# Batch 2's q in channel-major form, a new step list, and steps on other engines in an attention and gated-convolution kernel

## Chip, cores and metric

The kernel runs on 1 core of one Trainium2 chip. The metric is the device time of one execution in microseconds (us). A core has a matrix engine (PE, whose weight loads are shown apart as PEld), three elementwise engines (DVE, ACT, POOL) and SP, which here issues all the DMA transfers. Each engine takes its instructions strictly in the order of the program; engines wait for one another through semaphores.

## Reference

Eight batches, eight heads, 576 positions, 64 channels per head; everything is float32. A softmax of q over the channels of a head, a softmax of k over the positions, a 64x64 product per head, and then a causal convolution of five taps whose sigmoid gates a projection, followed by an output projection:

```python
q_s = np.exp(q - np.max(q, axis=-1, keepdims=True))
q_s = q_s / (np.sum(q_s, axis=-1, keepdims=True) + 1e-09)
k_s = np.exp(k - np.max(k, axis=2, keepdims=True))
k_s = k_s / (np.sum(k_s, axis=2, keepdims=True) + 1e-09)
kv = np.einsum('bhsd,bhse->bhde', k_s, v)
x = np.einsum('bhsd,bhde->bhse', q_s, kv)      # then (B, S, 512)
for j in range(5):
    gate_pre += conv_w[j][None, None, :] * xp[:, j:j + S, :]
gate = 1.0 / (1.0 + np.exp(-gate_pre))
out = (gate * (x @ w_val)) @ w_out
```

## The kernel before

The program is one list, ORDER (L31), of 973 steps such as "tap 1 3 0" (batch 1, block 3, tap 0). A loop at the end calls the function of each step, so the list alone sets the order of the instructions on every engine and of the DMAs on SP's queue. A letter at the end of a step names its engine: a is ACT, p is POOL, v is DVE. HOMES gives for each kind of buffer the sequence of buffers that its users take; a step that takes a buffer waits until all readers of its last user are done.

The 512 channels lie as 4 blocks of 128 partitions with the 576 positions along the free axis. Steps on PE, per batch: "kv b" (80 small matmuls), "attend b 0" and "attend b 1" (x of blocks 0, 1 and of blocks 2, 3), four "value b m" (24 matmuls each, x split into a high and a low part) and four "project b n" (24 matmuls each). PE writes to four PSUM banks, whose sequence is HOMES["bank"]. A bank is free again when its readers are done: for x they are x_high (L584), x_low (L597), first (L589), tap (L602) and far (L607); for a value block gated (L686); for a project block the copy to SBUF (L707). In a project the matmuls that need the block that was gated last come in the last quarter.

Between these: taps on DVE make the gate of a block, sigmoid (L616) on ACT, gated on DVE, then g_high and g_low split the product for project. x_low must have gone through all four blocks before the end of a batch's first value step, x_high before the parts that use it.

For q there are two ways. In batches 0, 1 and 2 q lies position-major; q_max, q_sub, q_exp, q_sum, q_eps, q_rec and q_mul normalise it, then PE transposes it (q_turn L542, 8 transposes each, twice a batch; tail_turn L556, 4 transposes for the last 64 positions of a pair of batches), and ACT copies it out (q_turned L553, tail_turned L562, tail_high L567). In batches 3 to 7 position-major q only yields the maximum plus the logarithm of the sum: q_total (L445, DVE), q_log (L451, ACT), l_turn (L455, one or two adds and four small transposes on DVE), l_row (L472, DMA to a row in DRAM), l_spread (L480, DMA of that row, repeated over partitions, into a buffer of q's kind). A second copy of q, channel-major from DRAM (load_qc L243), has this row subtracted (l_sub L488) and goes through the exponential (c_exp L492) straight into the form that attend reads. across (L240) says how many positions of a batch go this way: all 576 from batch 4 on, 512 in batch 3, whose last 64 come from the turn of the tail that batches 2 and 3 share.

At the start PE runs 24 warming matmuls (L724), while q and k of batch 0 and the packed weights (load_words, part, field, scaled, signed, joined, w_high, w_low: they unpack 64-bit words into two float parts) are made ready. The gates of blocks 0 and 1 of batch 0 are made on PE (conv, L663), which is the first long work after the warming.

## Time and profile before

| what | us |
|---|---|
| median of 3 runs (287.82 to 287.99) | 287.99 |
| the profiled execution | 287.65 |
| its span, first to last instruction | 285.9 |
| PE busy | 278.8 |
| PE weight loads busy | 250.6 |
| DVE busy | 231.7 |
| POOL busy | 205.8 |
| ACT busy | 192.8 |

The granted clock of PE was 1.00 throughout. Some 1.75 us of the profiled execution lie outside its span. Busy shares are averages over the span; the kernel has a start of about 27 us, a long middle in which all batches overlap, and a last part in which only PE has much to do. So the waits of PE and the share of each engine by stretch say more than the totals.

### The profile page before, as it was taken

To read this page: it belongs to the slowest core of one execution; us is meant where nothing else is said; L and a number is where in the kernel's file an instruction comes from. 1 tells how busy PE (TensorE), PEld (TensorE's weight loads), DVE (VectorE), ACT (ScalarE), POOL (GpSimd) and SP (SyncE) were. 2 spreads that over 40 slices of the span, in tenths; PEclk is the share of its full clock that TensorE was granted. 3 is DMA by queue.
4 is the path that set the end of the run, shared out by engine and by line. 5 is a ranking of instruction groups with operands and counts; after the bars stand their busy time and mean duration, and the time that the engine had idled before them with its cause. 6 is when DMAs were issued, how large, how long until landed. Compare 5 with 4: busy or idle time off the path is not lost.

```text
span 285.9 us, 6653 instructions
## 1 busy us (share of the span) xinstructions
PE 278.8 (98%) x2640; PEld 250.6 (88%) x2640; DVE 231.7 (81%) x329; ACT 192.8 (67%) x322; POOL 205.8 (72%) x191
## 2 busy tenths in 40 slices
...
GB/s 241 397 414 399 316 226 301 214 416 346 84 262 345 250 284 128 332 198 224 371 417 257 211 225 322 287 165 126 153 182 159 217 0 2 44 41 85 0 83 85
DMA packets 23463, 62.93 MB, mean 220 GB/s; under 512 B 3432, under 2 KB 3976, under 8 KB 20744
## 3 DMA queue, kind: packets, MB, share of 16 engines
...
q8 instruction: 21, 0.34, 0.5%
...
## 4 chain that ended last, share of the span: by engine, by line
PE 84%; DVE 7%; ACT 2%; issue 1%; POOL 1%; DVEq 0%
PE val L630 36%; PE out_a L630 32%; PE kv L521 6%; PE x L580 5%; PE cv L676 2%; DVE gate L605 2%; DVE x L600 1%; PE qTps L546 1%; DVE e L292 1%; DVE kpk L340 1%; PE kps L387 1%; ACT q L506 1%; PE out_r L630 1%; PE out_l L630 1%; POOL f L295 0%
## 5 line engine op out<-in xcount | busy, mean ns | idle before, releaser
L630 PE MATMUL val<-x,w_val_hi 128*128 128x288 f32 x512 | 89.1, 295 | 0.1
L605 DVE SCALAR_TENSOR_TENSOR gate<-x,cw,gate 128x575 f32<-128x575 f32 (+3 forms) x98 | 78.8, 809 | 5.7 <-ACT gate L593 2.2
L630 PEld LDWEIGHTS val<-x,w_val_hi 128*128 128x128 f32 x512 | 75.3, 188 | 0.3 <-DVE x L600 0.3
L630 PE MATMUL val<-x,w_val_lo 128*128 128x288 f32 x256 | 56.1, 300 | 0.0
L630 PE MATMUL out_a<-gh,w_out_lo 128*128 128x288 f32 x248 | 54.6, 301 | 0.0
L630 PE MATMUL out_a<-gh,w_out_hi 128*128 128x288 f32 x248 | 53.2, 296 | 0.0
L697 POOL TENSOR_TENSOR gl<-g,gh 128x576 fp32r<-128x576 f32 x24 | 34.6, 1443 | 14.7 <-ACT gh L198 8.0
L630 PEld LDWEIGHTS out_a<-gh,w_out_lo 128*128 128x128 f32 x248 | 39.4, 188 | 5.7 <-issue 1.8
L630 PE MATMUL out_a<-gl,w_out_hi 128*128 128x288 f32 x248 | 43.0, 295 | 0.0
L614 POOL TENSOR_TENSOR gate<-gate,far 128x572 f32<-128x572 f32 (+3 forms) x22 | 29.1, 1324 | 18.7 <-DVE gate L605 10.0
L630 PEld LDWEIGHTS val<-x,w_val_lo 128*128 128x128 f32 x256 | 40.7, 188 | 1.6 <-DVE g L689 0.4
L630 PEld LDWEIGHTS out_a<-gh,w_out_hi 128*128 128x128 f32 x248 | 39.8, 188 | 0.0
L204 ACT ACTIVATE o<-out_a 128x576 f32<-128x576 f32 x27 | 17.6, 650 | 31.6 <-PE out_a L630 22.0
L630 PEld LDWEIGHTS out_a<-gl,w_out_hi 128*128 128x128 f32 x248 | 36.4, 188 | 0.0
L420 POOL TENSOR_TENSOR q<-q,qm 128x512 f32<-128x512 f32 x32 | 33.5, 1062 | 3.6 <-DVE qm L415 3.5
L689 DVE SCALAR_TENSOR_TENSOR g<-gate,val 128x576 f32<-128x576 f32 x32 | 23.8, 749 | 13.8 <-PE val L630 5.9
L490 POOL TENSOR_TENSOR qc<-qc,lb 128x576 f32<-128x576 f32 (+1 forms) x17 | 24.1, 1428 | 11.0 <-DMA lb<-lrow 11.0
L355 POOL TENSOR_TENSOR k<-k,kmax 128x512 f32<-128x512 f32 x23 | 30.2, 1330 | 0.2
L617 ACT ACTIVATE gate<-gate 128x576 f32<-128x576 f32 x30 | 20.2, 683 | 8.3 <-DVE gate L605 8.0
L600 DVE TENSOR_TENSOR x<-x,x 128x576 fp32r<-128x576 f32 x32 | 23.1, 749 | 1.7 <-ACT x L198 1.6
L610 ACT ACTIVATE far<-x,cw 128x572 f32<-128x572 f32 (+3 forms) x22 | 16.2, 737 | 9.2 <-PE x L580 4.0
L424 ACT ACTIVATE q<-q 128x512 f32<-128x512 f32 (+2 forms) x11 | 15.9, 1442 | 8.8 <-POOL q L420 8.8
...
## 6 DMA issues: line engine op xcount, KB each, us to landing
...
lb<-lrow SPq DMA_DIRECT2D x8, 576.0 KB, 5.7
...
```

Of the source, the lines that this page charges most:

```text
L204: nc.scalar.mul(out, in_, factor)
L355: engine(e).tensor_sub(kk[r, cs], kk[r, cs], mx[r, cs])
L420: engine(e).tensor_tensor(qq, qq, m, op=ALU.add if b < 2 else ALU.subtract)
L490: engine(e).tensor_sub(t, t, T["lb", b][:, p])
L521: nc.tensor.matmul(acc[h * D:(h + 1) * D, p, :], T["k", b][:, c, cs] if c < 4 else ktz[b % 2][:, cs], T["v", b][:, c, hd] if c < 4 else T[ ...
L600: nc.vector.tensor_sub(xl, T["x", b, p], T["xh", b, p].bitcast(F32))
L605: nc.vector.scalar_tensor_tensor(out=a, in0=x, scalar=w, in1=a, op0=ALU.mult, op1=ALU.add)
L614: nc.gpsimd.tensor_add(a, a, T["far", b, p, j])
L617: nc.scalar.activation(T["gate", b, p], T["gate", b, p], AF.Tanh, scale=0.5)
L630: nc.tensor.matmul(ps[:, cs], a[:, kb, ms], z[:, cs], start=(i == 0), stop=(i == len(parts) - 1))
L689: nc.vector.scalar_tensor_tensor(out=T["g", b, m], in0=T["gate", b, m], scalar=1.0, in1=T["val", b, m], op0=ALU.add, op1=ALU.mult)
L697: engine(e).tensor_sub(T["gl", b, m], T["g", b, m], T["gh", b, m].bitcast(F32))
```

## The change

Batch 2 takes the second way: its q_sum, q_eps, q_rec, five q_mul, two q_turn, two q_turned, tail_turn, tail_turned and tail_high are gone, and so is tail_high of batch 3; load_qc, l_sub and c_exp (four each), q_total, q_log, l_turn, l_row and l_spread of batch 2 are new. across gives 576 from batch 2 on, so batch 3's four channel-major blocks grow from 512 to 576 columns. The list has another order (974 steps), and 90 of the steps that both have stand on another engine. The channel-major blocks and other users of the "f" buffers have 9 buffers where they had 6, the transposed q has 2 with a sequence of their own where it had 1, and the program reserves less memory for DMA (dynamic_dma_scratch_size). A second, identical definition of warm goes. The diff, cut to the parts of the list that are spoken of (the first of the removed lines begin at the second attend of batch 1):

```diff
-    load_km 5 0, tap 1 1 0, load_k 3, tap 1 1 2, put 0 1, part 7 a, x_low 1 1, signed 7, copy 0 0 a a, attend 1 1,
-    project 0 2, sigmoid 1 0, far 1 2 2, x_high 1 2 a, x_high 1 3 a, joined 7 p, w_high 7 a, q_sub 2 1 p, tap 1 1 3,
-    first 1 3 a, tap 1 1 1, sigmoid 1 1, w_low 7 p, k_spread 2, q_sub 2 0 p, k_sub 2 3 p, k_sub 2 1 p, k_peak 3 0,
-    k_peak 5 0, k_sub 2 0 p, copy 0 2 a a, load_v 3, tap 1 3 3, x_low 1 3, x_low 1 2, value 1 0, q_exp 2 0 5, put 0 0,
-    first 1 2 a, q_max 3 0 4, load_km 3 1, project 0 3, k_sub 2 4 p, gated 1 0, copy 0 3 a a, q_sum 2 0 5,
-    q_eps 2 0 5 a, load_km 3 3, value 1 1, k_sub 2 2 p, put 0 2, load_km 4 3, k_peak 3 3, kt_exp 2, load_km 4 2,
-    load_km 4 1, load_vt 2, k_peak 3 1, q_rec 2 0 5, k_row 3, k_exp 2, tap 1 2 0, load_km 4 0, tap 1 2 3, q_mul 2 4 a,
-    q_mul 2 1 a, gated 1 1, tap 1 2 1, tap 1 3 2, tap 1 3 0, tap 1 3 1, sigmoid 1 3, g_high 1 0 p, load_km 5 1,
-    q_sub 3 2 p, k_peak 4 3, value 1 3, kv 2, kv_sums 2, kv_norm 2 v, tail_turn 2, tail_turned 2 a, q_sub 3 0 p,
-    k_peak 4 2, g_high 1 1 a, q_mul 2 2 p, q_mul 2 0 p, q_mul 2 3 p, q_turn 2 0, q_sub 3 1 p, g_low 1 0 p,
-    q_turned 2 0 a, q_sub 3 3 p, k_peak 4 1, near 1 2 2, k_peak 5 3, put 0 3, gated 1 3, value 1 2, g_low 1 1 p,
-    q_exp 3 0 4, q_turn 2 1, k_spread 3, k_peak 5 1, k_peak 4 0, sigmoid 1 2, gated 1 2, tail_high 2 a,
-    q_turned 2 1 a, q_total 3, attend 2 0, far 2 1 0, first 2 0 v, tap 2 0 1, load_km 5 2, q_log 3, load_v 4,
...
+    load_words 3, load_taps, part 3 a, field 3 v, tap_field v, tap_scaled v, tap_signed, load_q 0 2 5, load_q 0 1 2,
+    load_kc 0 0, tap_part a, tap_joined p, scaled 3 a, signed 3, joined 3 p, w_high 3 p, warm 12, q_max 0 2 3,
+    q_sub 0 2 p, load_kc 0 2, q_max 0 3 5, q_each 0 4, q_sub 0 3 p, q_max 0 1 2, q_sub 0 1 p, k_top 0 0, k_raise 0 0,
+    load_kc 0 3, load_kc 0 1, load_ident, diag p, q_exp 0 3 4, k_top 0 2, q_exp 0 2 3, load_words 1, load_words 0,
+    load_q 0 0 1, load_km 2 0, field 1 p, scaled 1 p, k_top 0 3, k_top 0 1, q_sum 0 2 5, k_raise 0 3, part 1 v,
+    q_eps 0 2 5 v, q_max 0 0 1, k_raise 0 2, k_turn 0 1, q_exp 0 1 2, load_km 2 2, load_vt 0, load_v 0, k_raise 0 1,
+    k_turn 0 0, field 0 p, k_turned 0 1 a, q_each 0 0, signed 1, scaled 0 p, signed 0, load_km 2 1, part 0 a,
+    q_rec 0 2 5, k_tail_turn 0, q_sum 0 0 2, q_eps 0 0 2 v, q_rec 0 0 2, conv_rows, q_mul 0 4 p, q_mul 0 3 p,
+    k_peak 2 2, load_words 2, q_mul 0 0 p, load_q 1 0 5, k_turned 0 0 a, k_peak 2 0, k_tail_turned 0 a, q_mul 0 1 a,
+    tail_turn 0, k_peak 2 1, kv 0, tail_turned 0 a, tail_high 0 a, part 2 a, q_mul 0 2 v, q_turn 0 0, field 2 p,
+    load_kc 1 0, load_kc 1 3, scaled 2 a, kv_sums 0, q_turned 0 0 a, joined 1 p, w_high 1 a, w_low 1 p, joined 0 p,
+    kv_norm 0 v, conv_kv, q_turn 0 1, q_turned 0 1 a, load_kc 1 1, signed 2, joined 2 p, attend 0 0, x_high 0 1 a,
+    q_max 1 0 2, x_high 0 0 a, x_low 0 1, x_low 0 0, attend 0 1, tail_high 1 a, q_max 1 2 4, x_high 0 3 a, conv,
...
+    x_high 1 0 v, x_low 1 0, g_low 0 3 p, q_sub 2 3 p, project 0 0, first 1 1 a, tap 1 1 0, load_q 3 0 5, first 1 0 a,
+    joined 6 p, q_turned 1 1 a, copy 0 0 a a, load_qc 2 0, load_vt 2, tap 1 0 0, part 7 a, put 0 0, tap 1 0 3,
+    w_high 6 a, tap 1 0 2, load_km 3 2, q_sub 2 1 p, tap 1 0 1, q_max 3 0 4, k_spread 2, scaled 7 a, signed 7,
+    project 0 1, copy 0 1 a a, put 0 1, x_high 1 1 a, x_low 1 1, tap 1 1 3, w_low 6 p, attend 1 1, tap 1 1 2,
+    q_exp 2 0 5, first 1 2 a, joined 7 p, load_km 5 0, q_total 2, load_v 2, w_high 7 p, w_low 7 p, project 0 2,
+    copy 0 2 a a, x_high 1 2 a, q_sub 3 2 p, load_km 3 0, put 0 2, load_km 3 3, k_sub 2 3 p, tap 1 1 1, q_log 2,
+    l_turn 2, l_row 2, far 1 2 2, near 1 2 2, project 0 3, x_high 1 3 a, x_low 1 3, x_low 1 2, value 1 0, load_qc 2 1,
+    copy 0 3 a a, load_km 4 2, sigmoid 1 0, k_peak 3 2, k_peak 3 1, q_sub 3 3 p, sigmoid 1 1, k_sub 2 0 p, l_spread 2,
+    k_peak 3 0, value 1 1, first 1 3 a, tap 1 3 0, tap 1 3 3, gated 1 0, k_sub 2 2 p, k_sub 2 4 p, tap 1 3 2,
+    k_sub 2 1 p, tap 1 3 1, kt_exp 2, gated 1 1, k_peak 3 3, k_row 3, value 1 3, k_exp 2, q_sub 3 0 p, g_high 1 1 a,
+    sigmoid 1 3, tap 1 2 3, tap 1 2 1, load_qc 2 3, tap 1 2 0, kv 2, g_high 1 0 p, g_low 1 0 p, q_sub 3 1 p,
+    q_exp 3 0 4, gated 1 3, sigmoid 1 2, load_qc 2 2, load_km 4 1, l_sub 2 0 v, c_exp 2 0, kv_sums 2, kv_norm 2 v,
+    q_total 3, g_low 1 1 p, l_sub 2 1 p, l_sub 2 3 p, g_high 1 3 a, k_spread 3, value 1 2, gated 1 2, c_exp 2 1,
+    attend 2 0, x_high 2 0 a, first 2 0 a, x_high 2 1 v, x_low 2 1, g_low 1 3 p, g_high 1 2 p, g_low 1 2 p,
+    k_sub 3 2 p, project 1 0, first 2 1 v, tap 2 1 2, x_low 2 0, q_log 3, l_turn 3, put 0 3, copy 1 0 a a, tap 2 0 3,
+    k_peak 4 1, load_qc 3 0, far 2 1 3, near 2 1 3, tap 2 1 1, k_sub 3 0 p, load_q 4 0 5, q_max 4 0 5, c_exp 2 3,
+    l_sub 2 2 p, far 2 1 0, near 2 1 0, project 1 2, k_sub 3 1 p, put 1 0, k_sub 3 3 p, copy 1 2 a a, q_sub 4 1 p,
+    project 1 3, c_exp 2 2, copy 1 3 a a, far 2 0 0, load_qc 3 2, tap 2 0 2, l_row 3, tap 2 0 1, attend 2 1,
...
 HOMES = {
+    "f": "01234567831425067138467538043756418207153246170328456053",
+    "q": "01010101010010",
     "bank": (
-        "012303102130231213213120130212310101023023102021303013021312303013012303012323021312310101231230"
-        "101203032012303013230123012"
+        "012301231320123132132131032101300202301230320313123012323102020312030310202103232130202013021313"
+        "012120210303021310310231"
-    "q": "0101010101101",
-    "f": "0123451410153204524102541035203214502130142452301254",
+    "qT": "01010101",
...
 
     def across(b):
-        return S if b > 3 else MAIN
+        return S if b > 1 else MAIN
 
     def load_qc(b, p):
 
@@ -547,7 +548,7 @@
 
     def q_across(b):
         if ("qT", b) not in T:
-            T["qT", b] = work.tile([P, NB, S], F32, tag="qT", name=f"qT_{b}")
+            T["qT", b] = home(work, [P, NB, S], F32, "qT", f"qT_{b}")
         return T["qT", b]
 
     def q_turned(b, g, e="a"):
@@ -715,11 +716,6 @@
 
     def put(b, n, h="a"):
         nc.sync.dma_start(out=out[b, n][:, piece(h)], in_=T["o", b, n][:, piece(h)])
-
-    def warm(n):
-        ps = bank("warm")[:D, :512].rearrange("p (n d) -> p n d", d=D)
-        for _ in range(n):
-            nc.tensor.matmul(ps, ones, ones.unsqueeze(1).broadcast_to([P, 512 // D, D]), start=True, stop=True)
 
     def warm(n):
         ps = bank("warm")[:D, :512].rearrange("p (n d) -> p n d", d=D)
@@ -790,7 +786,7 @@
         "in_conv_w": np.ascontiguousarray(np.asarray(moe_conv_w).view(np.int64).reshape(TAPS, NB, P).transpose(2, 1, 0)).reshape(P, NB * TAPS),
         "in_ident": np.concatenate([np.eye(P, dtype=np.float32), np.tile(np.eye(D, dtype=np.float32), (2, 1))], axis=1),
     }
-    nc = bacc.Bacc("TRN2", target_bir_lowering=False, num_devices=1)
+    nc = bacc.Bacc("TRN2", target_bir_lowering=False, num_devices=1, dynamic_dma_scratch_size=1024)
     args = []
     for n, a in arrays.items():
         t = nc.dram_tensor(n, a.shape, mybir.dt.from_np(a.dtype), kind="ExternalInput").ap()
```

## Rows read from the trace of the kernel before

**Rows 1.** Waits of PE: engine and line, releaser, us in total, times, longest.

```profile
PE cv L676 <- DVE x L600: 1.1, 1, 1.1
...
PE rows L654 <- DVE k L200: 0.9, 1, 0.9
PE kps L387 <- ACT kc L380: 0.5, 1, 0.5
PE x L580 <- ACT qT L198: 0.5, 2, 0.2
```

**Rows 2.** The chain that ended last, in order of time: start, us, what.

```profile
27.47 5.73 PE cv L676 x80
...
68.77 0.53 PE val L630 x2
...
81.39 0.59 PE qTtps L560 x4
81.97 0.88 PE qTps L546 x8
...
86.20 0.87 PE qTps L546 x8
...
281.13 1.59 PE out_l L630 x12
```

**Rows 3.** Windows: stretch, length, then busy us of each engine, PE's clock, DMA.

```profile
27.40:70.00 42.60, 42.25 (x427) 37.23 (x428) 41.98 (x60) 38.01 (x81) 35.96 (x35) 1.00 0.86 306
70.00:100.00 30.00, 30.00 (x302) 28.07 (x301) 29.39 (x40) 24.99 (x45) 26.93 (x24) 1.00 0.75 239
100.00:200.00 100.00, 100.00 (x968) 94.62 (x968) 88.41 (x125) 70.64 (x93) 87.71 (x74) 1.00 0.79 253
200.00:286.00 86.00, 82.71 (x765) 78.89 (x763) 51.88 (x76) 38.64 (x59) 37.08 (x29) 1.00 0.28 88
```

**Rows 4.** Timeline of ACT: start, us, line, operation, tiles, count, idle before.

```profile
8.64 0.63 ACT L424 ACTIVATE q<-q 128x512 f32<-128x512 f32 x1 [3.68 <-POOL q L420]
...
25.50 1.19 ACT L198 CAST x<-x 128x576 fp32r<-128x576 f32 x2
...
89.06 1.28 ACT L453 ACT_TABLE_LOAD   x1
```

**Rows 5.** Groups of instructions by form, ACT, DVE and POOL: count, busy us, mean ns.

```profile
L204 ACT ACTIVATE o<-out_a 128x576 f32<-128x576 f32 x27 | 17.6, 650 | 31.6 <-PE out_a L630 22.0 <-issue 7.9 <-ACT gate L617 1.0
L198 ACT COPY qT<-qTps 128x1024 f32<-128x1024 f32 x6 | 6.0, 1017 | 0.3 <-PE qTps L546 0.3
...
L600 DVE TENSOR_TENSOR x<-x,x 128x576 fp32r<-128x576 f32 x32 | 23.1, 749 | 1.7 <-ACT x L198 1.6
...
L490 POOL TENSOR_TENSOR qc<-qc,lb 128x576 f32<-128x576 f32 x13 | 18.9, 1467 | 11.0 <-DMA lb<-lrow 11.0
```

**Rows 6.** Timeline of DVE: start, us, line, operation, tiles, count.

```profile
5.73 0.43 DVE L291 TENSOR_SCALAR e<-e 128x512 int32<-128x512 int32 x1 [5.73 <-POOL e L206]
...
26.67 1.41 DVE L600 TENSOR_TENSOR x<-x,x 128x576 fp32r<-128x576 f32 x2
...
67.31 1.41 DVE L600 TENSOR_TENSOR x<-x,x 128x576 fp32r<-128x576 f32 x2
68.64 2.27 DVE L415 TENSOR_REDUCE qm<-q 128x32 f32<-128x2048 f32 x1
...
71.49 2.81 DVE L430 TENSOR_REDUCE qs<-q 128x40 f32<-128x2560 f32 x1
...
87.24 2.28 DVE L449 TENSOR_REDUCE qs<-q 128x32 f32<-128x2048 f32 x1
...
92.95 0.84 DVE L465 STREAM_TRANSPOSE lt<-lse 32x32 f32<-32x32 f32 x4
```

**Rows 7.** Timeline of SP's queue, the spreading of batch 3's row.

```profile
97.15 1.33 SPq L486 DMA_DIRECT2D lb<-lrow  x2
```

**Rows 8.** The page's DMA issues: count, KB each, median us to landing.

```profile
lb<-lrow SPq DMA_DIRECT2D x8, 576.0 KB, 5.7
```

**Rows 9.** Line 697 on DVE: duration ns min/median/max, first and last start.

```profile
L697 DVE TENSOR_TENSOR gl<-g,gh x8: 745/758/1967, 54.3 to 271.3; 128x576 fp32r<-128x576 f32 x8
```

196 lines of the change are left out of this document (89 added, 107 removed).

## The prediction

> **What bounds the kernel now.** I read the waits of PE first [rows 1]. It waits in four places that matter, 3.0 us together, and all of them lie in the start or at the first attends. The chain of waits [rows 2] shows the same: conv begins at 27.47 and the last matmul ends at 281.13 + 1.59 = 282.72, and the windows between [rows 3] have PE busy for 42.25 of 42.60, 30 of 30 and 100 of 100 us. So from 27.5 us on the time is the sum of PE's own work, 255.25 us of it; a step taken from PE there is worth its full length as long as nobody makes PE wait. About 4.9 us lie behind the last matmul and around the span (287.65 - 282.72), the same in both kernels.
>
> Next I asked how near the others are. DVE is busy for 41.98 of 42.60 us up to 70 us and 29.39 of 30 up to 100; after that it has 11.6 us to spare in a hundred, then 34 in the last 86 [rows 3]. And at one place it is level with PE: x_low 1 3 and x_low 1 2 run from 67.31 to 68.72 [rows 6], and the chain passes to PE's value 1 0 at 68.77 [rows 2]. DVE is thus the second bound until 100 us, without margin near 69 us.
>
> **Part 1, what PE no longer does.** q_turn 2 0, q_turn 2 1 and tail_turn 2 stand in the chain with 0.88, 0.87 and 0.59 us [rows 2]. All three go: -2.34 us. Nothing is added to PE; batch 3's attends write all 576 columns before and after.
>
> **Part 2, the row of batch 2 in place of the turns.** ACT loses two copies of 1.02 us [rows 5], the tail's copies and sixteen small multiplies, and gains four exponentials and a logarithm. The logarithm needs a table load of 1.28 us; in batch 3 it began at 89.06, while q_total still ran on DVE from 87.24 to 89.52 [rows 4, 6], so most of it lies under the sum it waits for. ACT is no bound here: cost nothing, covered by its 5 idle us of 30 [rows 3], at worst 2 x 1.28 if that cover is gone. The Trainium skill (ScalarE: Activation LUTs, What ACT_TABLE_LOAD costs) puts a switch at 2.66 us with a drain; by that l_turn 2 would start some 1.3 us later, which the slack of the next paragraph still holds.
>
> The row itself must arrive. In batch 3 the last transpose ended at 92.95 + 0.84 = 93.79, the two spreading DMAs were issued from 97.15 to 98.48 and land 5.7 us later [rows 6 to 8]: 104.2, that is 10.4 us after l_turn. l_turn 2 stands just after tap 1 1 1, near 71 us by the walk below, so the row is there at 81 to 82. attend 2 0 is due near 86 (88.20 before, less the turns) and needs l_sub 2 1 on POOL, 1.47 us [rows 5], and an exponential before it: 2 us of slack. On SP the spreading waits for l_row 2, which waits for DVE; load_qc 2 3, load_qc 2 2 and k_row 3 are queued behind it. Cost nothing; if it comes late, PE loses each further us in full.
>
> **Part 3, the start.** PE's first long step, conv, needs a bank that x_low 0 1 frees, and that needs x_high 0 1 on ACT, which ran at 25.50 as the first of two [rows 4]. ACT has been without a break since 8.64. In the new list ACT carries 3.7 us of other steps up to there (k_turned 0 1, k_tail_turned 0, part 0, three short ones) and loses 2.2 (part 1, two scaled, a q_eps), net +1.6; of this scaled 3 and tap_part, 0.8, fall into the 3.68 us that ACT idled before its first exponential [rows 4]. That leaves 0 (DVE had x_low only at 26.67, 0.6 us after x_high 0 1 [rows 4, 6]) to +0.8. I take +0.3, nearer to the hidden end. The last block of q comes after two weight slabs now; if it came over 2 us later than its place in the list, the start would move (rival 2).
>
> **Part 4, the order around batch 1.** The bank sequence gives project 0 3 the bank of project 0 2, with no PE step between. PE must wait until copy 0 2 has emptied it: 0.65 us on ACT [rows 5] and the two handovers, 0.8 in all. Before, such pairs had an attend or a whole block between them. Bounds: 0 if DVE holds PE up at the next step anyway, 0.95 if ACT is a little late. I take +0.8.
>
> Right behind stands value 1 0 with its x_low 1 2. I summed DVE's list up to it, at one price of 0.75 per block step [rows 5]. Ahead of it now come q_max 3 0 4 (2.27), q_total 2 (2.81) [rows 6] and l_turn 2 (1.5, from 0.84 for four transposes [rows 6] and the adds), four block steps (3.0) and short ones (1.9): 11.4. Gone or moved behind are nine steps, one double (7.2). Net +4.2. Against that value 1 0 now follows project 0 3, one project later: 3.2 us, twice the 1.59 of the last half [rows 2]; the wait for the bank gives 0.8; and 0.9 (field 3, the taps) falls into the 5.73 us that DVE idled first [rows 6]. 4.2 against 4.9: value 1 0 finds its x_low just in time. Bounds -0.7 to +1.5 (the price per step is 5 to 10% loose over a list of 66 us). I take 0 there and +0.2 for the further handovers of batch 1, which are as close.
>
> **Part 5, ninety steps on another engine.** By the letters DVE takes over, net, three g_low, two l_sub, a k_sub and a q_mul (seven steps with two SBUF inputs), four copies of the output, an x_high and five g_high, gives up three first, three copies of k and a joined, and gets l_turn 2: ten block steps more at 0.75 [rows 5] and 1.5, some 9 us. POOL and ACT get lighter. Counted through the list, DVE has 1.4 us less than before up to attend 2 1, but 5.5 more up to project 4 0, near 200 us, and the rest behind, where it had 34 us to spare [rows 3]. So some 6.5 us fall into the 11.6 that it had between 100 and 200. Cost nothing with this cover; without it, 6.5.
>
> The trace shows what can eat the cover: the eight g_low on DVE took 0.745 at best, 0.758 in the median and 1.967 at worst [rows 9]. The Trainium skill (SBUF — State Buffer, SBUF: two separate sides) has a rule for it that speaks against this part: a DVE instruction with two SBUF inputs and a GpSimd instruction that reads SBUF share a port pair under an exclusive lock, and the later one waits for the whole of the other. By that rule each of the seven could wait; by the median few do.
>
> The larger pool of buffers and the smaller DMA reserve cost nothing and let loads start earlier; DMA moves some 2.6 MB more (four blocks of q, one spread row), at 239 GB/s and a share of 0.75 in that stretch [rows 3] it has the room.
>
> **Sum** against the profiled execution: 287.65 - 2.34 + 0.3 + 0.8 + 0.2 = 286.6. Later small waits in the stretch from 100 to 200 us, where DVE's spare time falls to about 3 us (part 5), I put at +0.1. That is 286.7, or -0.95 on the span's own time. The median of the runs lies 0.34 above the profiled execution (287.99 to 287.65), so 287.0.
>
> **Rivals**, as medians.
> 1. The full gain: the wait for the bank is taken from time that PE would lose to DVE anyway, and the start does not move; only the turns count: 287.99 - 2.34 = 285.65, to 286.2 with small waits. For it: PE's spare waits before 27.5 us [rows 1], 3 us that a better start could take back. Against it: two PE blocks in a row in one bank.
> 2. No gain: ACT's longer list (+0.8) and the late block of q (+0.6) move conv by 1.4, and the bank takes 0.8: 287.99 - 2.34 + 2.2 = 287.9.
> 3. Slower, DVE becomes the bound between attend 2 1 and project 4 0. 6.5 us more fall there (part 5) and PE comes 2.34 earlier: 11.6 - 6.5 - 2.3 = 2.8 spare [rows 3]. By the spread of line 697 each of the seven additional two-input steps may take up to 1.2 us longer [rows 9], 8.4 in all. From 2.8 on, a third of that, PE waits; at two thirds it waits 2.8 and the time is 287.0 + 2.8 = 289.8, at half 288.4. For it: DVE's 98% up to 100 us. Against it: median 0.758 on that line, so most such steps were not held up. The lock that the Trainium skill describes (SBUF — State Buffer, as above) would be its mechanism.
> 4. The change does only half of what it says: the turns go, but the row lands late and attend 2 0 waits. From 4 us late on it is slower than before; 1.5 us late gives 288.5.
>
> **How the numbers follow.** Forecast (286.3 to 287.8): 0.45; rival 1: 0.20; rival 2: 0.15; rival 3: 0.15; rival 4: 0.05. 0.2% is 0.58 us, about what a measurement here can tell from no change. Faster than 287.41: three quarters of the forecast and rival 1, 0.54. Within: a quarter of the forecast, most of rival 2, 0.24. Slower: 0.22. The range, 285.4 to 289.2, takes in rival 1 and rival 3 to its middle; the forecast's own range is given above.
>
> **What would show it.** PE with 48 - 16 turns of q; one wait of 0.7 to 0.95 us of PE at project 0 3 for copy 0 2 on ACT; conv starting between 27.3 and 28.3; attend 2 0 ending near 87, against 88.20; no DMA named before l_sub 2; windows of PE full from 100 on. It is wrong if PE loses over 1 us in all behind 100 us (rival 3, DVE named), if conv starts after 28.5 (rival 2) or if no wait stands at project 0 3.

## The result, and the profile after

The changed kernel takes 291.36 us (four runs, 290.40 to 291.72) where the kernel before takes 287.90 (four runs, 287.73 to 287.99): 1.0114 times as long [1.0097, 1.0132] (this ratio is worked out over the runs; the two medians by themselves give 1.0120). The prediction was 287.0, so 4.4 us are missing. The profiled execution took 291.72 us, its span is 289.9.

The windows of the kernel after come first (time of each stretch, then busy time of PE, its weight loads, DVE, ACT and POOL, granted clock, DMA share, GB/s); they answer to [rows 3].

```profile
0.00:27.40 27.40, 21.85 (x152) 12.07 (x152) 18.64 (x35) 18.54 (x44) 15.97 (x26) 0.94 0.93 346
27.40:70.00 42.60, 40.77 (x429) 34.17 (x428) 41.54 (x57) 38.88 (x82) 34.59 (x32) 1.00 0.79 271
70.00:100.00 30.00, 29.79 (x286) 28.69 (x287) 28.92 (x44) 22.89 (x30) 27.17 (x24) 1.00 0.84 236
100.00:200.00 100.00, 99.19 (x963) 92.58 (x962) 90.92 (x129) 69.30 (x94) 76.88 (x64) 1.00 0.87 278
```

PE is no longer full from 27.4 us on: 40.77 of 42.60 where it had 42.25, and 99.19 of 100 where it had 100. DVE has 91 of 100 us behind 100 where it had 88. The first stretch has a granted clock of 0.94. The waits of PE (line, what it waited for: us in all, times, longest) answer to [rows 1]:

```profile
PE qTtps L561 <- POOL q L509: 2.6, 1, 2.6
PE kps L388 <- ACT kc L381: 2.0, 1, 2.0
PE out_a L631 <- POOL w_out_lo L329: 1.2, 1, 1.2
...
PE x L581 <- ACT qT L494: 0.5, 1, 0.5
PE out_a L631 <- DVE g L690: 0.2, 1, 0.2
```

To add these up by place I walked through PE's timeline in both kernels. From the start of each kv and attend I took off PE's own work ahead of it in the list, at one price for each kind of step in both (3.20 for 24 matmuls, 2.68 for kv, 1.33 for attend, 0.88 and 0.59 for the turns). What is left is the time that PE has lost so far; only differences of it mean something.

| lost by PE up to | before | after | more |
|---|---|---|---|
| attend 0 0 | 2.61 | 6.09 | 3.48 |
| kv 1 | 3.50 | 6.20 | 2.70 |
| attend 1 1 | 3.80 | 7.05 | 3.25 |
| attend 2 1 | 4.06 | 8.88 | 4.82 |
| attend 5 0 | 4.06 | 10.42 | 6.36 |
| attend 7 1 | 4.05 | 10.42 | 6.37 |

6.37 lost, less the 2.34 of the turns, is 4.03; the two profiled executions differ by 291.72 - 287.65 = 4.07. So the three stretches hold all of it: 2.7 us up to kv 1, 2.1 from there to attend 2 1, 1.5 from there to attend 5 0, nothing behind.

**The start.** PE's timeline of the kernel after, from the end of the rows for conv (start, us, line, tile, count, idle time before and what ended it):

```profile
17.52 0.77 PE L655 MATMUL rows<-dg,ones 64*64 64x320 f32 x8
20.88 0.65 PE L561 MATMUL qTtps<-ident,q 128*128 128x128 f32 x4 [2.59 <-POOL q L509]
21.46 1.12 PE L522 MATMUL kv<-v,k 128*64 128x65 f32 x16
22.36 0.44 PE L522 MATMUL kv<-vt,ktz 128*64 128x65 f32 x4
22.58 1.09 PE L522 MATMUL kv<-v,k 128*64 128x65 f32 x16
...
25.52 1.97 PE L547 MATMUL qTps<-ident,q 128*128 128x128 f32 x16
```

PE stands idle for 2.6 us, and then kv 0 takes 4.06 us (21.46 to 25.52) where other kv steps take 2.48. The window over it shows why, in its last figures but two:

```profile
21.00:25.60 4.60, 4.60 (x85) 4.37 (x86) 2.73 (x5) 4.27 (x13) 4.00 (x4) 0.63 1.02 410
```

The granted clock is 0.63: for most of kv 0 PE ran at 1.2 instead of 2.4 GHz, after it had stood idle. Nothing of the kind is in the kernel before, whose clock was 1.00 throughout and whose longest idle gap of PE behind conv_rows is 1.1 us.

kv 0 also began 1.9 us later (21.46, before 19.55), and most of that was there before ACT's list had begun. The first maximum of q on DVE, before and after, and ACT's first exponential after:

```profile
6.80 1.80 DVE L415 TENSOR_REDUCE qm<-q 128x8 f32<-128x512 f32 x2
```

```profile
8.12 2.51 DVE L416 TENSOR_REDUCE qm<-q 128x8 f32<-128x512 f32 x3 [1.18 <-DMA q<-in_q]
10.07 2.02 ACT L500 ACTIVATE q<-q,qm 128x64 f32<-128x64 f32 x8 [4.36 <-DVE qm L416]
```

DVE waited 1.18 us for the first block of q, and ACT's list began at 10.07 instead of 8.64, 1.4 us later. From there to kv 0 it took 11.4 us, 0.5 more than before (10.9). So the 3.5 us that are lost more at attend 0 0 are some 1.4 for the late q, 0.5 for the longer list and 1.6 for the length of kv 0; 0.8 of them come back by kv 1, since the wait of 1.1 us at conv [rows 1] is nearly gone. In the changed list load_taps goes out ahead of that block of q, which is issued at 1.65 instead of 1.15. In the fourteen profiles with the changed start the first maximum begins between 7.45 and 8.55, in the six with the old start between 6.80 and 7.27. No run moved this load alone, so its share of the start is read from the traces and not shown by an experiment.

**Batch 1.** DVE and then POOL ahead of project 0 3, which begins at 70.21 after a wait of 1.17 us for w_low 7:

```profile
63.42 2.28 DVE L416 TENSOR_REDUCE qm<-q 128x32 f32<-128x2048 f32 x1
65.61 0.42 DVE L292 TENSOR_SCALAR e<-e 128x512 int32<-128x512 int32 x1
66.06 0.69 DVE L293 SCALAR_TENSOR_TENSOR e<-words,e 128x512 int32<-128x512 int32 x1
```

```profile
66.84 1.30 POOL L296 TENSOR_TENSOR f<-e,f 128x512 int32<-128x512 int32 x1 [1.90 <-DVE e L293]
68.20 0.61 POOL L201 CAST w_out_hi<-f 128x512 fp32r<-128x512 f32 x1
68.89 1.26 POOL L329 TENSOR_TENSOR w_out_lo<-f,w_out_hi 128x512 fp32r<-128x512 f32 x1
```

signed 7 stands behind q_max 3 0 4 on DVE, POOL idles 1.90 us for it, and joined 7, w_high 7 and w_low 7 follow without a break to 70.15. Copy 0 2, which I had expected here, ran from 69.13 to 69.78: the bank came free inside the same wait.

```profile
69.13 0.65 ACT L205 ACTIVATE o<-out_a 128x576 f32<-128x576 f32 x1 [0.52 <-ACT gate L594]
```

No wait of PE stands at value 1 0.

**The row at attend 2 0.** The row of batch 2 was issued at 76.73 and landed at 82.87, 6.1 us later. These are the last exponential of its first half on ACT and the attend on PE:

```profile
88.74 0.68 ACT L494 ACTIVATE qT<-qc 128x576 f32<-128x576 f32 x1
89.30 1.36 PE L581 MATMUL x<-qT,kvd 64*64 64x288 f32 x16
```

PE does not wait for the row. But it came 3.3 us later than the 86 at which attend 2 0 was due, and the exponential ended at 89.42, when the attend had already begun. The 2 us of slack that the prediction counted on were not there: l_sub 2 0, at 85.88 on DVE, stood behind gated 1 3. That no wait is named at this place owes something to luck.

**Between 100 and 200 us.** ACT ahead of attend 4 0 (152.20, a wait of 0.5 for the exponential):

```profile
145.76 0.32 ACT L454 ACTIVATE qs<-qs,eps 128x32 f32<-128x32 f32 x1 [1.29 <-DVE qs L450]
149.02 1.28 ACT L618 ACT_TABLE_LOAD   x1 [2.94 <-DVE gate L606]
150.31 0.69 ACT L618 ACTIVATE gate<-gate 128x576 f32<-128x576 f32 x1
150.90 1.24 ACT L494 ACTIVATE qT<-qc 128x576 f32<-128x576 f32 x2
```

ACT stands 2.94 us before sigmoid 3 3 for taps on DVE, then loads the table, and the two exponentials of attend 4 0 are queued behind it.

### The profile page after: what moved, and what is told of

Read it like the earlier page. It is cut to its first block, busy times and chain, and to the rows that moved or that the text cites. A ratio compares the mean times of both kernels' runs of the same rounds, so it can differ in the third digit from the quotient of the medians.

```text
span 289.9 us, 6607 instructions
## 1 busy us (share of the span) xinstructions
PE 278.3 (96%) x2620; PEld 250.4 (86%) x2620; DVE 242.6 (84%) x351; ACT 191.1 (66%) x306; POOL 197.7 (68%) x176
## 4 chain that ended last, share of the span: by engine, by line
PE 66%; DVE 20%; DMA 5%; ACT 3%; issue 3%; POOL 1%; SPq 1%; DVEq 0%; ACTq 0%; POOLq 0%
PE val L631 28%; PE out_a L631 27%; DVE gate L606 6%; PE kv L522 5%; DMA q<-in_q 5%; PE x L581 5%; DVE qm L416 3%; DVE x L601 2%; DVE g L690 2%; DVE e L293 1%; DVE kpk L341 1%; DVE ktop L377 1%; DVE e L292 1%; DVE qs L450 1%; ACT qT L199 1%
## 5 line engine op out<-in xcount | busy, mean ns | idle before, releaser
L606 DVE SCALAR_TENSOR_TENSOR gate<-x,cw,gate 128x573 f32<-128x573 f32 (+3 forms) x98 | 78.2, 810 | 6.7 <-ACT gate L594 3.0
L698 POOL TENSOR_TENSOR gl<-g,gh 128x576 fp32r<-128x576 f32 x21 | 30.3, 1450 | 16.3 <-DVE gh L201 11.1
L421 POOL TENSOR_TENSOR q<-q,qm 128x512 f32<-128x512 f32 x32 | 32.9, 1043 | 3.8 <-DVE qm L416 3.8
L356 POOL TENSOR_TENSOR k<-k,kmax 128x512 f32<-128x512 f32 x22 | 28.5, 1312 | 0.4 <-DMA kmax<-krow 0.4
L491 POOL TENSOR_TENSOR qc<-qc,lb 128x576 f32<-128x576 f32 x19 | 27.9, 1487 | 1.2 <-DMA qc<-in_q_channels 1.1
L205 ACT ACTIVATE o<-out_a 128x576 f32<-128x576 f32 x23 | 15.0, 651 | 20.5 <-PE out_a L631 17.4
L199 ACT CAST x<-x 128x576 fp32r<-128x576 f32 x25 | 15.8, 641 | 13.3 <-PE x L581 10.0
L416 DVE TENSOR_REDUCE qm<-q 128x8 f32<-128x512 f32 (+3 forms) x12 | 20.9, 1746 | 1.3 <-DMA q<-in_q 1.2
```

Source lines behind the costliest of these rows:

```text
L199: nc.scalar.copy(out=out, in_=in_)
L356: engine(e).tensor_sub(kk[r, cs], kk[r, cs], mx[r, cs])
L416: nc.vector.tensor_reduce(out=T["qm", b][:, cs], in_=qq, axis=AX.X, op=ALU.max, negate=b < 2)
L421: engine(e).tensor_tensor(qq, qq, m, op=ALU.add if b < 2 else ALU.subtract)
L491: engine(e).tensor_sub(t, t, T["lb", b][:, p])
L606: nc.vector.scalar_tensor_tensor(out=a, in0=x, scalar=w, in1=a, op0=ALU.mult, op1=ALU.add)
```

## The experiments

Eighteen kernels were run; none is as fast as the kernel before. The columns of losses are worked out as above for the profiled execution of each, which can lie up to 2.5 us from its median (e4b: 292.77 against 290.22); DMA landings at the start differ from execution to execution, by 1.1 us in the first maximum of q. The slower matmuls of a lower clock are in them.

| run | median us | ratio to before | lost up to kv 1 | kv 1 to attend 2 1 | behind |
|---|---|---|---|---|---|
| kernel before | 287.9 | 1 | 3.5 | 0.6 | 0 |
| changed kernel | 291.36 | 1.0114 [1.0097, 1.0132] | 6.2 | 2.7 | 1.5 |
| e1_rec_early | 291.40 | 1.0138 [1.0097, 1.0179] | 6.2 | 2.5 | 1.5 |
| e2_v_early | 291.29 | 1.0103 [1.0067, 1.0139] | 5.8 | 2.8 | 1.5 |
| e3_rec_and_v | 292.36 | 1.0159 [1.0128, 1.0190] | 5.6 | 2.9 | 3.8 |
| e4_filled_gap | 292.21 | 1.0149 [1.0132, 1.0166] | 6.5 | 2.7 | 1.5 |
| e4b_filled_gap_half | 290.22 | 1.0093 [1.0078, 1.0108] | 5.6 | 3.0 | 1.5 |
| e5_old_start | 290.36 | 1.0099 [1.0078, 1.0120] | 5.0 | 2.6 | 1.5 |
| e6_words_bank | 293.99 | 1.0211 [1.0187, 1.0236] | 6.7 | 5.2 | 1.5 |
| e6b_words_alone | 293.96 | 1.0219 [1.0196, 1.0242] | 8.0 | 3.3 | 1.5 |
| e7_engines_100_200 | 308.50 | 1.0721 [1.0688, 1.0753] | 6.3 | - | - |
| e8_turns_back | 297.35 | 1.0333 [1.0311, 1.0356] | 6.5 | 6.0 | 1.4 |
| e9_row_alone | 303.09 | 1.0547 [1.0521, 1.0574] | 3.5 | 16.9 | 0.8 |
| e9b_row_alone | 298.93 | 1.0380 [1.0357, 1.0403] | 3.6 | 10.2 | 3.0 |
| e10_old_to_attend | 293.46 | 1.0190 [1.0171, 1.0209] | 3.7 | 7.1 | 1.6 |
| e11_gap_and_table | 289.69 | 1.0067 [1.0049, 1.0085] | 5.2 | 2.5 | 0.7 |
| e12_sum_first | 293.21 | 1.0185 [1.0171, 1.0199] | 4.7 | 5.8 | 0.6 |
| e13_old_start_mended | 292.82 | 1.0179 [1.0166, 1.0193] | 4.8 | 6.1 | 0.7 |
| e14_less_dve | 291.01 | 1.0114 [1.0087, 1.0141] | 7.3 | 2.5 | 1.5 |
| e15_less_dve_bank | 291.17 | 1.0120 [1.0105, 1.0135] | 4.4 | 2.2 | 1.5 |

### The gap in the start: two loads and a queue

e1 moves two steps on DVE, e2 two loads on SP, e3 does both:

```diff
-    q_sum 0 2 5, k_raise 0 3, part 1 v, q_eps 0 2 5 v, ... signed 0, ... q_rec 0 2 5,
+    q_sum 0 2 5, q_eps 0 2 5 v, q_rec 0 2 5, k_raise 0 3, part 1 v, ... signed 0, ...
-    load_q 0 0 1, load_km 2 0, ... load_km 2 2, load_vt 0, load_v 0,
+    load_q 0 0 1, load_vt 0, load_v 0, load_km 2 0, ... load_km 2 2,
```

> The changed kernel with one edit on DVE: q_eps 0 2 5 and q_rec 0 2 5 come right behind q_sum 0 2 5, ahead of the last block's q_max and of part 1, signed 1 and signed 0. In the changed kernel PE stood idle for 2.6 us ahead of tail_turn 0 (20.88), which waits for q_mul 0 4 on POOL, and so for q_rec. Theory A (DVE's queue behind the late block of q costs the start): tail_turn 0 at 18.3, kv 0 2.2 earlier at normal speed, conv some 2 us earlier, time 289.3. Theory B (the load of v, issued at 12.46 and landing 8.8 us later, at 21.3, is a second bound that ends at the same time): tail_turn 0 goes to 18.3, but kv 0 still starts near 21.3, and the time stays within 0.3 of the changed kernel's 291.4. Theory C (ACT's longer list sets the start): no change either, kv 0 early but conv not.

> The changed kernel with one edit on SP's queue: load_vt 0 and load_v 0 go out ahead of two blocks of k (load_km 2 0 and 2 2, 576 KB). v should land near 19.5 where it landed at 21.3. Theory A: tail_turn 0 at 20.9 as before and so no gain, 291.4. Theory B: no gain alone either, as tail_turn 0 still comes first; both have to be mended. If the time falls by over 1 us here alone, both A and B are wrong, and v alone was the bound.

> Both edits: q_rec 0 2 5 right behind its sum on DVE, and v ahead of two blocks of k on SP. Theory B (two bounds that end together): kv 0 starts near 19.5 and takes 2.5 to 3 us where it took 4.06, conv starts near 28.5, where it started at 30.48, and the time is about 289.5. Theory A: the same as with the first edit alone. Theory C (ACT's list): kv 0 early, but conv within 0.5 us of 30.48.

No gain from any. With q_rec early tail_turn 0 did move to 18.25, but the wait moved with it to kv 0, and not to v as theory B had it:

```profile
PE kv L518 <- ACT k L195: 2.6, 1, 2.6
```

The trace names ACT's copies of k as what releases kv 0 there, at 21.47, the same time as in the changed kernel. But v landed at 21.33 and the copy ended at 21.36, so the trace can hardly tell the two apart, and theory B's figures came true. So three things ended within 0.3 us of one another: q through DVE, v, and ACT's list. With q_rec and v both early kv 0 came 0.6 us earlier (20.89), released by ACT (2.5 us of wait). ACT's list had begun 0.5 us earlier too in that execution (9.55 against 10.07), because the first block of q had landed sooner, so the two edits by themselves show no gain. Theory C is nearest: ACT's list is what kv 0 waits for in the end. Its start, which follows the first block of q, is the larger part of the delay, and its greater length some 0.5 us. In e3 the 0.6 were lost again behind 100 us, where ACT waited 3.3 us for an output buffer whose last store had not yet ended.

### The clock over kv 0

e4 and e4b put 13 and 6 matmuls into the gap behind conv_rows:

```diff
+    def fill(n):
+        for _ in range(n):
+            nc.tensor.matmul(T["rows"][:D, TAPS * D:512], ones, ones.unsqueeze(1).broadcast_to([P, 3, D]), start=True, stop=True)
-    conv_rows, q_mul 0 4 p,
+    conv_rows, fill 6, q_mul 0 4 p,
```

> The changed kernel with 13 small matmuls on PE behind conv_rows, into columns of that bank that nobody reads (their result is not used). They fill the gap of 2.6 us ahead of tail_turn 0, and nothing else is changed. The clock granted from 21.0 to 25.6 us was 0.63 in the changed kernel, and kv 0 took 4.06 us there, 2.48 elsewhere. Theory D (the idle gap lets the clock fall, and 1.5 us of the start are that): kv 0 starts near 21.5 as before, at full clock, takes 2.5, conv starts 1.3 to 1.5 earlier, time 290.0. Rival: the clock falls for another reason, or kv 0's length is covered by ACT: 291.4.

> The run with the filled gap again, with 6 instead of 13 matmuls: those took 4.44 us, twice the gap, so that kv 0 began 1.9 us late (though at full clock, 2.48 us); 6 of them take 2.05 and fit into the gap of 2.6 us. Theory D (the clock at its lower level costs the start 1.5 us): kv 0 begins at 21.5 and takes 2.5, attend 0 0 moves from 27.7 to 26.4, the time lost up to kv 1 falls from 6.2 to 5, and the time to 290.1. Rival (DVE and ACT behind it are as late): kv 0 short, but the loss at kv 1 and the time as in the changed kernel.

PE's timeline of e4 shows the size missed and the mechanism confirmed:

```profile
18.43 4.44 PE L656 MATMUL rows<-ones 128*64 128x192 f32 x26
22.80 0.66 PE L558 MATMUL qTtps<-ident,q 128*128 128x128 f32 x4
23.39 0.69 PE L519 MATMUL kv<-v,k 128*64 128x65 f32 x16
...
25.87 1.97 PE L544 MATMUL qTps<-ident,q 128*128 128x128 f32 x16
```

Each of the 13 is two instructions of 0.17 us, so they took 4.44 us and kv 0 began 1.9 us late; yet it took 2.48 (23.39 to 25.87), and attend 0 0 came only 0.35 us later than in the changed kernel. With 6 the median was 290.22, where theory D had 290.1 and the changed kernel has 291.36; but the intervals of the two ratios overlap (to 1.0108 and from 1.0097), so the medians alone don't show a gain. In the profiled execution of e4b q came later still: kv 0 began at 22.26 and the loss up to kv 1 was 5.6, not the 5 that theory D had.

What shows the cost of the clock is the stretch from the start of kv 0 to the start of conv. It took 9.02 us in the changed kernel, 9.02 in e1 and 8.97 in e14, where the clock fell over kv 0, and 7.44 in e4, 7.59 in e4b and 7.59 in e2, where it stayed at 1.00: 1.4 us. (In e3 it stayed at 1.00 and the stretch took 9.02, because PE waited there for q on DVE and for ACT, 0.8 us each.) The whole times point the same way. Among the twelve executions of e14 and e15, which have one list up to conv, the four with a mean clock of 1.000 took 289.42 to 290.57 and the eight at 0.994 took 290.89 to 292.67. The four of the changed kernel are too few for it: 290.40 at 1.000, but 291.62 at 0.998, beside 291.09 and 291.72 at 0.994.

What decides whether the clock falls isn't settled. Ten profiles with the changed start have the gap of 2.4 to 3.3 us unfilled; the clock fell in seven of them and not in e2, e3 and e15. In the four with a filled gap it stayed at 1.00. This is e2, where PE stood still for 3.2 us at the same place:

```profile
21.00:25.60 4.60, 3.69 (x90) 3.46 (x91) 4.27 (x10) 4.54 (x13) 4.06 (x5) 1.00 1.02 415
```

### The old start, and the old list up to attend 1 0

e5 takes the steps up to conv in the order, on the engines and in the banks of the kernel before; e10 those up to attend 1 0.

> The changed kernel from conv on, with the start of the kernel before: its order of steps up to conv, its engines for them, its order of loads there and its sequence of banks. The four runs before this one mended one wait each of the changed start and moved attend 0 0 by at most 0.6 us, since three things release kv 0 within 0.3 us of one another (the last block of q through DVE, the load of v, ACT's copies of k). Theory A (the start as a whole, order and loads together, costs what the trace says): the PE time lost up to kv 1 falls from 6.2 to 3.5 us, and the time by 2.7, to 288.7. Rival (given back): DVE or the loads behind conv were as late and hold PE up at kv 1 or attend 1 1 instead; 290 to 291.

> The changed kernel from attend 1 0 on, the list of the kernel before up to there (order, engines, loads, banks), for those steps that both have up to there. With the old list up to conv alone attend 0 0 came 3.0 us earlier, but 1.9 of that was lost again by kv 1, to waits of PE for x_low on DVE. Theory A (that was the seam between the two lists, and the whole stretch up to attend 1 0 belongs together): PE's loss at attend 1 0 is 3.8 where the changed kernel had 6.5, the time 2.7 less, 288.6. Theory B (DVE has more to do from batch 1 on in the changed list, and gives the gain back wherever the seam lies): loss at kv 2 over 7.5, time 290 or more.

In e5 attend 0 0 came 3.0 us earlier, but 1.8 of it was gone by kv 1: PE waited at the seam for x_low on DVE.

```profile
PE val L628 <- DVE x L598: 1.3, 1, 1.3
...
PE cv L674 <- DVE x L598: 1.1, 1, 1.1
```

The second stands in the kernel before too [rows 1]; the first is new. In e10 the seam lay at attend 1 0. The loss at kv 1 was 3.7 (the kernel before has 3.5), but at attend 1 0 it was 5.0 where theory A had 3.8, and 5.4 us were lost between kv 1 and attend 1 1. So e5 came out as its rival had it (given back, 290 to 291) and e10 as theory B: in both, what stands behind the seam in the changed list did not follow the earlier start. Only 1.0 us was left of e5's gain by the medians, and the ratios of e5 and the changed kernel overlap.

### Words and bank at project 0 3

```diff
-    tap 1 0 1, q_max 3 0 4, k_spread 2, scaled 7 a, signed 7,
+    tap 1 0 1, scaled 7 a, signed 7, q_max 3 0 4, k_spread 2,
```

e6b does this alone; e6 also puts tap 1 1 1 behind tap 1 1 2 and exchanges banks 0 and 2 from project 0 3 on.

> The changed kernel with two edits around project 0 3. scaled 7 and signed 7 come ahead of q_max 3 0 4 in the list, so w_low 7 should end 2.2 us earlier; and project 0 3 takes the bank of block 1 of batch 1 (its last tap, tap 1 1 1, comes ahead of q_total 2 for it), value 1 0 that of project 0 2, so that no project follows another in one bank. In the changed kernel PE waited 1.17 us there for w_low 7, and the bank would have come free 0.9 us into that wait. Theory A (two bounds, words and bank, that end together, and nothing behind them): the wait goes, time 1.1 less, 290.2. Theory B (DVE is the bound around batch 1): PE waits as long for x_low 1 2 at value 1 0, or at the next gated, and the time stays at 291.3.

> The changed kernel with scaled 7 and signed 7 ahead of q_max 3 0 4, and the banks as they are there. w_low 7 should end some 2 us earlier. Theory A (the bank of project 0 2 is a bound of its own, and comes free at 69.9): PE still waits 0.8 to 0.95 us at project 0 3, now for copy 0 2 on ACT, and the time lost at kv 2 falls by 0.25. Theory B (words alone): no wait at project 0 3, 1.1 us less. Theory C (DVE is the bound there, and any step put earlier makes another later): the wait moves to x_low 1 2 or to the taps, no gain or a loss of up to 1 us.

Both are 2.6 us slower. By the profiled executions most of e6b's share is the start, where kv 0 ran wholly at the lower clock (0.50 from 22 to 26 us) and 8.0 us were lost up to kv 1 instead of 6.2; from attend 1 1 to kv 2 it lost 2.4, 0.7 more than the changed kernel. e6 lost 4.3 there, 2.6 more. The waits of e6b at this place, then that of e6:

```profile
PE out_a L628 <- ACT o L202: 0.9, 1, 0.9
...
PE val L628 <- DVE gate L603: 0.5, 1, 0.5
...
PE val L628 <- DVE g L687: 0.2, 1, 0.2
```

```profile
PE out_a L628 <- DVE gate L603: 2.3, 1, 2.3
```

With the words early the bank is the bound, with 0.9 us: the wait that the prediction named, hidden so far behind a longer one. And behind it DVE is late. With the bank taken from block 1 of batch 1 PE waits 2.3 us for that block's last tap on DVE. So e6b has the wait that theory A names and the balance that theory C names, and e6 came out as theory B.

### Is it DVE's work?

e12 is e11 (below) with q_max 3 0 4 behind value 1 0 and the other bank; e13 has the same edits, the old start and an earlier x_low 0 2. e14 and e15 leave four taps out.

```diff
-    tap 1 0 0, part 7 a, put 0 0, tap 1 0 3, w_high 6 a, tap 1 0 2, load_km 3 2, q_sub 2 1 p, tap 1 0 1,
+    part 7 a, put 0 0, w_high 6 a, load_km 3 2, q_sub 2 1 p,
```

> The run with the filled gap and sigmoid 3 3 behind the exponentials (289.7), and in batch 1: q_max 3 0 4 (2.27 us of DVE) goes from ahead of signed 7 to behind value 1 0, q_sub 3 2 with it, and project 0 3 takes the bank of block 1 of batch 1, whose last tap comes ahead of q_total 2. That failed before while q_max 3 0 4 still stood ahead of those taps (a wait of 2.3 us of PE for a tap), and with the words alone PE waited 0.9 for the bank and 0.7 for DVE. Theory A (what costs batch 1 is the 2.27 us that the new list puts on DVE ahead of value 1 0): the loss from attend 1 1 to kv 2 falls from 1.65 to 0.5 or less, time 288.5. Theory B (all of DVE's work there is due at the same time): the loss shows again at gated 1 0 to value 1 3 or at the row, time 289.7 or more.

> The changed kernel with the old start up to conv (290.4 alone), x_low 0 2 right behind x_low 0 3 and k_peak 2 0 and 2 1 later, so that value 0 1 need not wait 1.3 us for DVE as it did at that seam; and the three edits of batches 1 and 3 of the run beside it, without the filled gap. Theory A (the losses of the start, of batch 1 and of ACT's list add up and can be taken away one by one): PE's loss at kv 1 is 3.7 to 4, 5.5 in all, 287.0, faster than the kernel before. Theory B (DVE is the bound up to kv 2 and what is won in one place is lost in the next): loss at kv 2 over 7, time 289 or more.

> The changed kernel without the four taps of block 0 of batch 1 (tap 1 0 0 to 1 0 3), so that the gate of that block has only its first term; nothing else is moved. They took 3.3 us of DVE between attend 1 0 and q_max 3 0 4. In the changed kernel the loss from attend 1 1 to kv 2 was 1.65, with 1.17 of it at project 0 3 for w_low 7. Theory A (DVE's work ahead of value 1 0 makes the words late; the bank that project 0 3 takes from project 0 2 is a bound of its own, 0.9 when the words were early): the wait at project 0 3 becomes one of 0.9 for copy 0 2 on ACT, the rest goes, the loss is 0.9 to 1.0 and the time 290.6. Theory B (not DVE but POOL or the loads): 1.65 and 291.3 as before.

> Again without those four taps, and project 0 3 in the bank of block 1 of batch 1, value 1 0 in that of project 0 2, as in the run that was slower for a tap's wait of 2.3 us. Theory A (two causes there: DVE's work and the bank): neither wait is left, the loss from attend 1 1 to kv 2 is 0.3 or less and the time 289.9. Theory B (the bank is not a cause, DVE alone is): the same as with the taps left out alone, 290.6 or whatever that gives.

In e12 and e13 the wait at project 0 3 shrank to 0.4 and came back at value 1 3, which needs the bank that gated 1 0 frees; here PE and then DVE of e12:

```profile
79.88 0.53 PE L627 MATMUL val<-x,w_val_lo 128*128 128x288 f32 x2 [2.03 <-DVE g L690]
```

```profile
73.33 2.27 DVE L412 TENSOR_REDUCE qm<-q 128x32 f32<-128x2048 f32 x1
75.53 2.06 DVE L337 TENSOR_REDUCE kpk<-km 128x1 f32<-128x576 f32 x3
77.51 1.65 DVE L602 SCALAR_TENSOR_TENSOR gate<-x,cw,gate 128x572 f32<-128x572 f32 x2
79.08 0.74 DVE L690 SCALAR_TENSOR_TENSOR g<-gate,val 128x576 f32<-128x576 f32 x1
```

Theory B again: DVE works without a break, and a step put later delays the one behind it. Whether the three k_peak could go behind gated 1 0 wasn't tried. With 3.3 us of taps left out the profile of e14 shows one wait at project 0 3, for copy 0 2:

```profile
71.04 0.50 PE L627 MATMUL out_a<-gh,w_out_lo 128*128 128x288 f32 x2 [0.88 <-ACT o L201]
```

and the loss from attend 1 1 to kv 2 is 1.35 where it was 1.65; with the other bank 1.06. So DVE's work and the bank are both causes, as theory A has it, but they explain 0.6 of the 1.65, not the 1.35 that it expected: 1.06 stay, 0.4 of it a wait for w_low 7 and 0.3 what the kernel before loses there too. The medians (291.01, 291.17) can't tell this; the start scatters by more.

### Engines and ACT's list behind 100 us

e7 takes the old engine for 27 steps between attend 2 1 and project 4 0. e11 is e4b with one step moved:

```diff
-    sigmoid 3 3, kv_norm 4 v, load_km 6 2, l_sub 4 1 p, c_exp 4 1, put 2 3, l_sub 4 0 p, c_exp 4 0, attend 4 0,
+    kv_norm 4 v, load_km 6 2, l_sub 4 1 p, c_exp 4 1, put 2 3, l_sub 4 0 p, c_exp 4 0, sigmoid 3 3, attend 4 0,
```

> The changed kernel with the engines of the kernel before for the 27 steps that changed engine between attend 2 1 and project 4 0; same order. This takes six steps net off DVE there, some 5 us of its 91 in the stretch from 100 to 200 us. PE lost 1.7 us in that stretch (attend 3 1, attend 4 0, 4 1 and 5 0). Theory A (the moved steps make DVE the second bound, rival 3 of the prediction): these losses go, 289.8. Theory B (they come from the order or the loads: the table of the logarithm ahead of sigmoid, kmax late for the tail of k): losses stay within 0.5, 291; or more, if ACT or POOL is now too slow.

> The changed kernel with the gap ahead of tail_turn 0 filled by 6 matmuls (290.2 alone), and sigmoid 3 3 on ACT behind c_exp 4 1 and c_exp 4 0. In the changed kernel ACT idled 2.94 us for the taps of that gate on DVE, then loaded the table (1.28), and only then came the two exponentials that attend 4 0 waits for: PE lost 0.5 there. Theory A (a wait in ACT's list, not DVE as a bound): the loss at attend 4 0 goes from 0.53 to 0.1 and the time to 289.7. Theory B (DVE as the bound between 100 and 200 us, rival 3): the loss comes back at the next project, where gated 3 3 is due, and the time stays at 290.2.

e7 took 17 us more, though DVE was lighter. Its windows and waits:

```profile
100.00:200.00 100.00, 90.89 (x843) 81.63 (x843) 74.16 (x106) 57.87 (x78) 70.45 (x59) 0.93 0.77 234
```

```profile
PE x L578 <- ACT qT L491: 6.6, 5, 1.8
...
PE out_a L628 <- POOL gl L695: 2.4, 3, 1.8
```

DVE is busy for 74 of 100 us, in part because PE got through less work in that window (843 matmuls where it had 963), and PE waits for POOL's g_low and for exponentials. These old engines don't fit the new order, and so e7 can't say whether DVE was the bound there; e11 can. It gave 289.69, as forecast (289.7). That is 0.53 less than e4b, but the ratios overlap; it is the trace that carries the reading: the wait at attend 4 0 is gone, and the loss behind attend 2 1 is 0.66 instead of 1.54. So more than half of what PE lost there was ACT's list. The loss did not come back at the next project, as rival 3 would have it.

### The change of batch 2 by itself

e8 puts the turns back into the changed list; e9 and e9b put the row into the list of the kernel before (e9 leaves one tap out of a gate, see the text on e9b).

> The changed kernel, its order and its engines, but batch 2's q goes position-major through PE again, as in the kernel before (q_sum, q_eps, q_rec, five q_mul, two q_turn, tail_turn and their copies; no row, no l_sub, no second copy of q; batch 3's last 64 positions from the turn of the tail). Theory A (the turns are worth their full length on PE, and the row costs nothing): 2.3 us slower than the changed kernel, 293.7. Theory B (the way by the row costs DVE and the loads as much as it saves PE): the same as the changed kernel, 291.3, or faster.

> The kernel before, its order and its engines, with the way by the row for batch 2 put into it and nothing else of the new list: the turns of batch 2 and what belongs to them go; q_total 2, q_log 2, l_turn 2, the two DMAs of the row, four loads of channel-major q, four l_sub and c_exp come in; some fifteen steps around them move by a few places so that the row can be there in time; the larger pool of buffers is the changed kernel's. Theory A (the change of batch 2 pays its 2.34 us of PE, and the new list is what costs): the time lost by PE stays near 4.1 us in all, 285.6 to 286.6. Theory B (the way by the row itself costs what it saves, through DVE's 1 us more, the row coming late at attend 2 0, or the loads): 287.5 to 289.

> Again the kernel before with the way by the row for batch 2 put into its list, since the first such list had a slip: sigmoid 1 1 stood ahead of a tap of the same gate, which left that tap out of the gate and made DVE wait 4.8 us for ACT. Now the order of taps and sigmoid is that of the kernel before; q_exp 2 0 5 comes 2 us earlier, the x_low pair ahead of q_total 2, the row's two DMAs ahead of the loads that can wait. Theory A (the change of batch 2 pays its 2.34 us, the new list is what costs): PE's loss stays near 4.1 to 4.6 us, 285.6 to 286.4. Theory B (the row takes 10 to 12 us from l_turn to its landing, so that it can't be there by attend 2 0, due at 84.7 in this list, unless batch 1 gives way): a wait of 1 to 3 us of PE at attend 2 0 for the exponential, 286.7 to 288.7, and none elsewhere. Theory C (DVE cannot take 1 to 2 us more ahead of attend 2 0): losses at value 1 1 to value 1 2, over 288.

With the turns back the changed list is 6.0 us slower, more than either theory had. 2.34 of it is PE's work, 3.4 are new losses up to attend 2 1, the largest kv 2 behind ACT's exponential of k and attend 2 0 behind the turns' copies. So in this list the way by the row pays at least what it takes off PE; but the list was made for the row, and the turns were put into it without making it anew. In the old list I did not find a place for it. e9b is 11 us slower than the kernel before. Its two longest waits of PE, and the step of DVE before the first of them:

```profile
82.92 0.75 DVE L686 SCALAR_TENSOR_TENSOR g<-gate,val 128x576 f32<-128x576 f32 x1
83.77 1.13 PE L518 MATMUL kv<-v,k 128*64 128x65 f32 x16 [4.40 <-issue]
105.27 0.70 PE L577 MATMUL x<-qT,kvd 64*64 64x288 f32 x2 [2.08 <-ACT qT L490]
```

The larger stands at kv 2. The trace names no releaser, but by HOMES kv 2 takes there the bank of value 1 1, whose reader gated 1 1 ended on DVE at 83.67, 0.1 us before; a q_max, k_peak steps and taps stand ahead of it. That is theory C. kv 2 then took 3.67 instead of 2.48 us, at a clock of 0.65. The other wait is not theory B's: it stands at attend 2 1. At attend 2 0, which began at 90.92, no wait of PE is named, though the row's DMAs were issued at 78.04 and POOL's l_sub at 88.10 waited 1.3 us for their landing; the attend took 1.77 us beside its exponentials. Both lists were made by hand, and their losses show that an order around attend 2 0 is hard to find, not that the row is dear. Whether the 4.4 us would go with fewer DVE steps ahead of gated 1 1 wasn't tried. Whether some order close to the old one gains 2.3 us stays open.

## Why the prediction was wrong

- **Part 1, the turns: right.** PE's work is 2.34 us shorter, and e8 shows it worth at least that in this list, which was not made for the turns.
- **Part 2, the row: right on the cost, in part by luck.** No wait of PE for the row stands at attend 2 0, and rival 4 did not come. But the slack was used up: the last exponential ended 0.1 us behind the start of the attend, which PE reached 3.3 us later than forecast. (Rival 4's two figures don't go together: 1.5 us late gives its 288.5, which is slower than before, so "from 4 us late on" is wrong.)
- **Part 3, the start: the step that failed most**, +0.3 put, +2.7 measured. ACT's longer list, which was the whole of the sum, took some 0.5, inside its bounds of 0 to 0.8 (as the figures stand, 3.7 less 2.2 is 1.5, not 1.6). The step that failed is that everything else was left as in the old trace. It kept ACT's first exponential at 8.64 and had no term for the first block of q, which landed later: it came at 10.07, 1.4 us later. And it had no term for the length of kv 0, which took 4.06 instead of 2.48 us, because PE stood idle for 2.6 us ahead of it and the clock fell; 1.4 us of that is still there at conv, by the runs with and without the fall. Against the kernel before, 0.8 came back at conv, which has its own wait there. I had read "the granted clock was 1.00 throughout" as a fact about the chip; it was a fact about a PE without long gaps. Conv began at 30.48, and the prediction said that after 28.5 it would be wrong. Why the first block of q lands later, and why the clock falls behind some gaps only, stays open.
- **Part 4, batch 1: the place was right, the cause only in part, and the sum too small**, +1.0 put, +2.1 measured. The wait at project 0 3 is there with 1.17 us where 0.8 was put, and its cause in the trace is w_low 7; the bank (0.88 to 0.9 in e6b and e14) lies inside it. The step on value 1 0 went by DVE's list as far as x_low 1 2 and came out, with no wait there; but it left out that signed 7, and so w_low 7, stands behind q_max 3 0 4 in the same list. The further handovers, put at 0.2, took some 0.9, in pieces that no wait names.
- **Part 5, ninety steps: right that DVE is no bound, wrong on the price**, +0.1 put, +1.5 measured. DVE has 90.9 us of 100, 2.5 more than before and not 6.5. The largest part of the loss came from ACT: sigmoid 3 3 waits for taps and holds two exponentials back, and 0.9 us went when it was moved (e11). I had called ACT no bound because it has 30 us to spare in a hundred; in this list the spare time lay in front of the sigmoid and not where the exponentials needed it. The prediction's sign of being wrong, over 1 us lost behind 100 us, came true, with ACT named in place of DVE. The table loads of the logarithm took 1.28 us each, as before; a switch of 2.66 us, which the Trainium skill (ScalarE: Activation LUTs, What ACT_TABLE_LOAD costs) gives, no row here shows. Of the port pair that, by the Trainium skill (SBUF — State Buffer, SBUF: two separate sides), a DVE step with two SBUF inputs and a GpSimd step that reads SBUF hold one after the other, the trace agrees in three cases of sixteen: the three such steps (g_low and l_sub) on DVE that took over 1 us (1.18, 1.68 and 1.97) all began while a step on POOL was running. One lies at a place that matters: l_sub 2 0 took 1.68 us at 85.88, beside POOL's l_sub from 85.51 to 86.94, where the median of five such steps is 0.75. Where the DVE step began first it took 0.70 to 0.76, and POOL's step beside it 1.81 and 1.95 instead of 1.43. With medians of 0.75 it cost DVE little.

The terms together: 286.7 + 2.4 (start) + 1.1 (batch 1) + 1.4 (behind) = 291.6, against 291.72 in the profiled execution. No rival alone was it. Rival 2 had the place of the start and half its price, and its mechanism only in part: ACT's list grew by 0.5 and not 0.8, and it was the first block of q that came late, not the last. Rival 3 had the sign, with the wrong engine.
